# Weights summed and split ahead and kept in DRAM, and seven products in two more token pairs: attention with two feed-forward networks on one core

## The chip, the core and the metric

The kernel runs on one core of one Trainium2 chip. The metric is device time in microseconds (us), from the start to the end of one execution. The engines are TensorE (PE, matrix products), VectorE (DVE), ScalarE (ACT), GpSimd (POOL) and SyncE (SP). PE, DVE and ACT compute here. SP and POOL hand out transfers between DRAM and the on-chip memory (SBUF), each from a queue of its own in the order in which the program lists them; POOL also issues transfers that add what they bring to what is there. PE writes to eight accumulator banks (PSUM) of 128 x 512 fp32.

## What is computed

The reference, cut to its core (N = 6016 tokens, C = 256, hidden width 2048, all fp32):

```
qn = q / (norm(q, axis=tokens) + 1e-6);  kn = k / (norm(k, axis=tokens) + 1e-6)
s  = kn.T @ qn / tau                     # 256 x 256
a  = softmax(s, axis=-1)
x  = v @ a                               # 6016 x 256
h  = x @ w_in;   x2  = silu(h) @ w_out
h2 = x2 @ w2_in; out = max(0.01 * h2, h2) @ w2_out
```

So there is a small attention over channels and then two feed-forward networks over all tokens. The weights come as 64-bit words and the kernel makes fp32 of them by itself ("decoding").

## The kernel before

**High and low parts.** Every fp32 matrix is split into a high part in a shorter fp32 format (an ACT cast) and a low part (a DVE subtraction). A product of two such matrices is three matmuls: high x high, high x low, low x high. Below, "a product" always means such three matmuls into the same bank.

**Token pairs and steps.** The tokens are cut into six pairs of blocks (`tpairs`): pairs 0 to 4 have two blocks of 512 columns, pair 5 two of 448. The hidden width is cut into eight steps a pair (`SS`), each with two 128-row halves of the hidden layer. A step is (network, pair, step), numbered k = 0 to 95; k = 0 to 47 is the first network. A group g of weights serves steps 2g and 2g + 1.

**Seven products for eight.** A step's first layer is a 2 x 2 block product of weights and tokens. Except in pair 0 of the first network (`first_plain`), `first_seven` computes it by Strassen-Winograd's scheme, with seven products M1 to M7 in place of eight, from sums of weights and sums of tokens that are made beforehand. The second layer is again a 2 x 2 block product. A plain second layer (`l2`) has eight products. `l2_seven` has seven (P1 to P7): it needs sums of the second layer's weights (`wo_sums`: s2, s3, s4 in the tiles `wsh` and `wsl`, and a21 replaced by a21 + a22), and sums of the activations, T1 and T2 on DVE, T3 and T4 as adding transfers on POOL (`onto_home`, L592). T4 feeds P4 and T3 feeds P7. P1, P5, P6 and P7 go through a bank of their own (`ps_x`) for two steps at a time (`BATCHES`), are kept in SBUF as E1 to E5 (`keep`, L684) and are added to the results at the end of the pair (`close`, L689). Which steps use it says `seven`: before, the second network's steps 0, 1, 2, 4, 5 and 6; steps 3 and 7 and the whole first network have plain second layers.

**Between the networks.** `finish` copies the first network's four results a pair (L703) and stores them in DRAM (`y_d`); `tokens` loads them when the second network needs them. In the second network `finish` transposes and stores the output.

**The weights of the second network.** The decoding is cut into jobs (`job_load`, `job_s0`, `job_s1a`, `job_s1`, `job_hi`, `job_lo`), one chain for all 32 pieces of both networks. The first 16 are the first network's: their high and low parts go straight to the weight tiles. The decoded words of the other 16 are stored to DRAM (`w2_d`, L329). From pair 5 of the first network on, `weights(g)` prepares group after group: SP reloads the words (`reload_w`, L1055), DVE makes the seven first-layer forms (`w_sum`, L116), ACT and DVE split them into `wch` and `wcl`; then the same for the second layer (`reload_wo`, L1067; `wo_sums`, L1090; `woh`, `wol`, `wsh`, `wsl`). Both use one buffer, `f`, one after the other.

**What sets the order.** For k < 8 the order is written out by hand. From K0 = 8 on, a planner in the program does it while the program is built: each piece of work is a `Work` with an engine, an estimated cost, what it depends on, a due time and an earliest step; the planner runs a little clock for each engine and lists the instructions in the order that results. `LATE` is how long after its issue it takes a result to be there: 3.0 us for an SP transfer, 4.2 us for one of POOL. On the chip each engine keeps that order, and waits in it for whatever isn't there. Blocks of 128 x 512 ("homes", `take`) are handed out from a list of 46, and of 49 from the second network on, when the buffers of the preparation are given back (`open_more`, `open_last`).

Of the kernel before, what the change touches and what calls it, by code (L numbers as in the profile page):

```python
# [8 lines left out]
F32 = mybir.dt.float32  # L9
F32R = mybir.dt.float32r  # L10
U32 = mybir.dt.uint32
# [8 lines left out]
def attention_moe_kernel(  # L20
# [44 lines left out]
    BATCHES = ((0, 1), (2, 4), (5, 6))  # L65
# [185 lines left out]
    w2_d = {}  # L251

    def w2i_piece(g, kc):
        w2_d["i", g, kc] = dram.tile([P, PW], F32, tag=f"w2i{g}{kc}", name="w2i_d")
        return w2_in[kc * P:(kc + 1) * P, g * GW:(g + 1) * GW, :], w2_d["i", g, kc]

    def w2o_piece(j):
        w2_d["o", j] = dram.tile([P, PW], F32, tag=f"w2o{j}", name="w2o_d")
        return rows(w2_out, 2 * j), w2_d["o", j]
# [52 lines left out]
    def job_s1():  # L312
        if at["s1a"] == at["s1"]:
            job_s1a()
        i = at["s1"]
        if i < at["s1a"]:
            w, r = words32[i]
            nc.vector.tensor_tensor(out=w, in0=w, in1=r, op=ALU.add)
            at["s1"] += 1

    def job_hi():
        i = at["hi"]
        if i < at["s1"]:
# [4 lines left out]
            else:  # L328
                nc.sync.dma_start(out=jobs[i][1], in_=w)  # L329
# [12 lines left out]
    phase = [0]  # L342
# [92 lines left out]
    def seven(step):  # L435
        return step[0] == 2 and any(step[2] in b for b in BATCHES)

    def batch(step):
        return next(b for b in BATCHES if step[2] in b)
# [246 lines left out]
    def close(p, m, half, name):  # L686
# [7 lines left out]

    CLOSE = ((0, 0, "E1"), (0, 1, "E2"), (1, 0, "E3"), (1, 1, "E3"), (0, 1, "E5"), (1, 1, "E5"))

    def finish(moe, p, m, half):
# [4 lines left out]
        if moe == 1:  # L702
            nc.vector.tensor_copy(out=o[:, :n], in_=ps)  # L703
# [15 lines left out]
    with tc.manual_schedule():  # L719
# [260 lines left out]
        plains = sorted(set(range(SS)) - {s for b in BATCHES for s in b})  # L980
        late = [s for b in BATCHES for s in b] + plains
# [70 lines left out]
        def reload_w(g):  # L1052
            wf[g] = new_f(7 * HG, "w_f").rearrange("p (i c) -> p i c", c=HG)
            for kc in range(KC):
                nc.sync.dma_start(  # L1055
                    out=wf[g][:, kc:kc + 3:2, :],
                    in_=w2_d["i", g, kc].rearrange("p (a b) -> p a b", a=2),
                )

        wo_f, wo_more = {}, {}  # L1060

        def reload_wo(g):
            a = new_f(FG * C + 6 * P, "wo_f")
            wo_f[g] = a[:, :FG * C].rearrange("p (f c) -> p f c", c=C)
            wo_more[g] = a[:, FG * C:]
            for x in range(2):
                nc.sync.dma_start(  # L1067
                    out=wo_f[g][:, 2 * x:2 * x + 2, :],
                    in_=w2_d["o", 2 * g + x].rearrange("p (f c) -> p f c", c=C),
                )  # L1070

        def wo_hi(g, s, eng="act"):
            hi_of(woh[g][:, s, :], wo_f[g][:, s, :], eng)

        def wo_lo(g, s):
            lo_of(wol[g][:, s, :], wo_f[g][:, s, :], woh[g][:, s, :])

        wo_s = {}

        def wo_sums(s):  # L1080
            g = s // 2
            f, fi = wo_f[g], s % 2
            wo_s[s] = wo_more[g][:, fi * 3 * P:(fi + 1) * 3 * P].rearrange("p (x c) -> p x c", c=P)
# [8 lines left out]
        def ws_hi(s, eng="act"):  # L1092
            wsh[s] = more_pool[0].tile([P, 3, P], F32R, tag=f"wsh{s}", name="wsh")
            wsl[s] = more_pool[0].tile([P, 3, P], F32R, tag=f"wsl{s}", name="wsl")
            hi_of(wsh[s], wo_s[s], eng)

        def ws_lo(s):
            lo_of(wsl[s], wo_s[s], wsh[s])
# [22 lines left out]
        def open_more():  # L1121
            decode.close()
            more_pool[0] = ctx.enter_context(tc.tile_pool(name="spool", bufs=1))
            fpool[0] = prepare.enter_context(tc.tile_pool(name="fpool2", bufs=1))

        prepare = ExitStack()

        def open_last():
            prepare.close()
# [334 lines left out]
```

## Time and profile before

| what | value |
|---|---|
| median of 3 runs | 1024.15 us (1023.77 to 1024.96) |
| the profiled execution | 1024.44 us |
| its span, first to last instruction | 1022.7 us |
| PE busy | 1010.3 us, 99% |
| DVE busy | 766.8 us, 75% |
| ACT busy | 727.2 us, 71% |
| POOL busy | 93.5 us, 9% |
| moved by DMA | 86.58 MB, 85 GB/s in the mean |

The attention and the first products end at about 75 us. The first network's pair 0 goes on to about 149 us, pairs 1 to 3 to 393.6, pair 4 to 475.2 and pair 5 to about 550. The second network's pairs follow at 78 us each. A share of busy time is a mean over such stretches; what an engine has to spare is read from the stretch in question.

### The profile page before, as it was taken

Reading aid. Unit: us, or ns where it says so; the run is one execution under the profiler, and the core shown is the slowest. Engines: PE = TensorE matmul, PEld = TensorE weight load, DVE = VectorE, ACT = ScalarE, POOL = GpSimd, SP = SyncE. Lnnn points to the kernel's source line nnn. Section 1 sums busy time; section 2 is a strip of 40 time slices with the busy share of each in tenths; the row PEclk is TensorE's granted clock in tenths of the full one; section 3 lists DMA queues with packets and bytes.
Section 4 is the critical chain, followed back from the end, with each engine's and each line's share of the span. In section 5 each row is a group of like instructions: output and inputs, shape, how many; then the busy total and the mean of one; then the engine's idle time right before and its main releaser. Section 6 shows DMA issues by size and latency. Waiting matters only on the chain.

```text
span 1022.7 us, 13051 instructions
## 1 busy us (share of the span) xinstructions
PE 1010.3 (99%) x4516; PEld 843.4 (82%) x4516; DVE 766.8 (75%) x1291; ACT 727.2 (71%) x1336; POOL 93.5 (9%) x109
## 2 busy tenths in 40 slices
PE   9999999999999999999999999999999999999997
PEld 8778888888888888888988778888888888888997
DVE  5889787656747655644777899879879879879886
ACT  7789756765766665755767887876876776877773
POOL 2200000000000000000000111211211211211110
PEclk9999999999999999999999999999999999999999
DMA  9723532214215214001212514623523623522433
GB/s 354 294 82 104 124 68 77 59 54 114 52 50 125 53 31 119 20 20 52 74 61 92 110 42 104 104 42 83 103 42 83 103 42 78 94 41 51 77 57 53
DMA packets 128914, 86.58 MB, mean 85 GB/s; under 512 B 94800, under 2 KB 101200, under 8 KB 128848
## 3 DMA queue, kind: packets, MB, share of 16 engines
q1 hardware_dynamic: 111888, 61.69, 21.3%
q0 software_dynamic: 13248, 23.60, 13.0%
q10 hardware_dynamic: 3712, 0.46, 0.3%
q8 instruction: 35, 0.57, 0.2%
q14 instruction: 31, 0.25, 0.1%
HBM read 45.61 MB, written 16.52 MB: 61 GB/s over the span
## 4 chain that ended last, share of the span: by engine, by line
PE 90%; DMA 4%; ACT 2%; DVE 2%; SPq 1%; issue 1%; DVEq 0%
PE ps_y L629 37%; PE ps_a L456 22%; PE ps_d L456 11%; PE ps_x L629 9%; PE ps_b L456 6%; PE ps_h L456 3%; DMA k_raw<-in_k_dram 2%; PE w_ps L368 1%; DMA q_raw<-in_q_dram 1%; DMA w_raw<-in_moe_w_in_dram 1%; DMA wo_f<-w2o_d 1%; SPq L751 0%; PE s_ps L764 0%; DMA w_f<-w2i_d 0%; ACT hs L467 0%
## 5 line engine op out<-in xcount | busy, mean ns | idle before, releaser
L483 DVE TENSOR_TENSOR gl<-hs,gh 128x512 fp32r<-128x512 f32 (+1 forms) x492 | 322.0, 675 | 84.3 <-ACT gh L122 79.8
L122 ACT CAST gh<-hs 128x512 fp32r<-128x512 f32 (+1 forms) x492 | 287.5, 612 | 10.5 <-PE ps_y L629 2.1
L629 PE MATMUL ps_y<-gl,woh 128*128 128x512 f32 (+1 forms) x552 | 212.8, 386 | 0.8 <-DVE gl L483 0.8
L629 PE MATMUL ps_y<-gh,wol 128*128 128x512 f32 (+1 forms) x552 | 212.8, 385 | 0.5 <-DVE wol L339 0.5
L629 PE MATMUL ps_y<-gh,woh 128*128 128x512 f32 (+1 forms) x552 | 212.8, 386 | 0.0
L456 PE MATMUL ps_a<-xh,wch 128*128 128x512 f32 (+1 forms) x352 | 136.3, 387 | 1.7 <-DVE ps_d L540 1.6
L456 PE MATMUL ps_a<-xl,wch 128*128 128x512 f32 (+1 forms) x352 | 135.6, 385 | 0.0
L456 PE MATMUL ps_a<-xh,wcl 128*128 128x512 f32 (+1 forms) x352 | 135.5, 385 | 0.0
L629 PEld LDWEIGHTS ps_y<-gh,wol 128*128 128x128 f32 x552 | 103.6, 188 | 20.4 <-DVE wol L339 1.0
L629 PEld LDWEIGHTS ps_y<-gl,woh 128*128 128x128 f32 x552 | 103.6, 188 | 20.3 <-DVE gl L483 1.2
L629 PEld LDWEIGHTS ps_y<-gh,woh 128*128 128x128 f32 x552 | 103.6, 188 | 19.9 <-DVE ps_y L689 0.8
L560 DVE TENSOR_TENSOR hs<-ps_a,c 128x512 f32<-128x512 f32 (+1 forms) x88 | 59.6, 677 | 68.5 <-PE ps_a L456 66.4
L592 POOL DMA_DIRECT2D hs<-hs x72 | 62.5, 929 | 363.3 <-DVE gl L483 96.6
L540 DVE TENSOR_TENSOR ps_d<-ps_a,c 128x512 f32<-128x512 f32 (+1 forms) x88 | 60.1, 684 | 47.2 <-PE ps_a L456 45.9
L467 ACT ACTIVATE hs<-ps_b 128x512 f32<-128x512 f32 (+1 forms) x40 | 23.5, 587 | 85.6 <-PE ps_b L456 83.1
L456 PEld LDWEIGHTS ps_a<-xh,wch 128*128 128x128 f32 x352 | 66.1, 188 | 16.9 <-DVE ps_d L540 3.6
L456 PEld LDWEIGHTS ps_a<-xh,wcl 128*128 128x128 f32 x352 | 66.1, 188 | 12.3
L456 PEld LDWEIGHTS ps_a<-xl,wch 128*128 128x128 f32 x352 | 66.1, 188 | 11.9
L456 PE MATMUL ps_d<-xh,wch 128*128 128x512 f32 (+1 forms) x176 | 67.9, 386 | 0.0
L456 PE MATMUL ps_d<-xl,wch 128*128 128x512 f32 (+1 forms) x176 | 67.8, 385 | 0.0
L456 PE MATMUL ps_d<-xh,wcl 128*128 128x512 f32 (+1 forms) x176 | 67.8, 385 | 0.0
L534 ACT COPY ps_b<-ps_a 128x512 f32<-128x512 f32 (+1 forms) x87 | 49.1, 565 | 24.7 <-PE ps_a L456 23.1
(139 smaller groups left out, 1631.3 us busy)
## 6 DMA issues: line engine op xcount, KB each, us to landing
hs<-hs POOLq DMA_DIRECT2D x60, 256.0 KB, 3.2
w_raw<-in_moe_w_in_dram SPq DMA_DIRECT2D x16, 512.0 KB, 4.4
w_raw<-in_moe_w_out_dram SPq DMA_DIRECT2D x16, 512.0 KB, 3.6
y_d<-o SPq DMA_DIRECT2D x20, 256.0 KB, 2.0
xf<-y_d SPq DMA_DIRECT2D x20, 256.0 KB, 3.6
out_dram<-o SPq DMA_DIRECT2D x80, 64.0 KB, 2.2
q_raw<-in_q_dram SPq DMA_DIRECT2D x9, 512.0 KB, 9.9
k_raw<-in_k_dram SPq DMA_DIRECT2D x9, 512.0 KB, 9.9
```

The source lines that it names most:

```text
L122: nc.scalar.copy(out=hi, in_=src)
L368: nc.tensor.matmul(ps, lhsT=a[:, jc, m * P:(m + 1) * P], rhs=b[jc], start=(x == 0), stop=(x == len(order) - 1),)
L456: nc.tensor.matmul(ps[:, :n], lhsT=a, rhs=b, start=(start and x == 0), stop=(x == 2), skip_group_check=not start,)
L467: nc.scalar.activation(out=h, in_=src, func=AF.Silu)
L483: nc.vector.tensor_tensor(out=lo[1], in0=h[1], in1=f32(got[0][1]), op=ALU.subtract)
L534: nc.scalar.copy(out=to, in_=got["A"][:, :n])
L540: nc.vector.tensor_tensor(out=got["D"][:, :n], in0=got["A"][:, :n], in1=got["c5"], op=ALU.add)
L560: nc.vector.tensor_tensor(out=hs[step, "22"][1], in0=got["A"][:, :n], in1=got["c5"], op=ALU.add)
L592: nc.gpsimd.dma_start(out=hs[step, part][1], in_=hs[step, "T2"][1], accum_op=ALU.add)
L629: nc.tensor.matmul(ps, lhsT=a, rhs=b, start=(first and x == 0), stop=(last and x == 2), skip_group_check=True,)
```

## The change

1. **Seven products in the first network's pairs 4 and 5.** `FIRST_SEVEN = 32`: `seven` now also takes the first network's steps from k = 32 on, with the same batches. `finish` adds one kept sum to each of the four results there, so that two of the six closes remain. Before pair 4's step x, `weights_first` replaces a21 by a21 + a22 in the first network's `woh` and `wol` and fills `wsh` and `wsl`, by transfers on POOL.
2. **The preparation is moved.** Decoded words of the second network go into the buffer `f` directly (`job_s1` writes there) and no longer to DRAM. While pairs 1 to 3 of the first network run, `prepare_in` and `prepare_out` make the sums and split everything through two homes at a time (`stage`), and SP stores the high and low parts in DRAM (`store`). The decoding is spaced 0.65 steps a half in place of one. The first network's second-layer words are stored too (`w1_d`, eight transfers in `job_hi`), loaded again (`reload_first`), summed and split (`prepare_first`).
3. **The weights are fetched ready-made.** `weights(g)` is now only transfers on POOL (`fetch`), two for each tile pair, straight into `wch`, `wcl`, `woh`, `wol`, `wsh` and `wsl`: 52 in all with those of the first network.
4. **Around it:** the three additional homes come with `open_more`, when everything is prepared. `LATE` of SP is 5.0 in place of 3.0.

The core of the diff:

```
-    BATCHES = ((0, 1), (2, 4), (5, 6))
+    FIRST_SEVEN = 32
+    BATCHES = {1: ((0, 1), (2, 4), (5, 6)), 2: ((0, 1), (2, 4), (5, 6))}
...
     def seven(step):
-        return step[0] == 2 and any(step[2] in b for b in BATCHES)
+        moe, p, s = step
+        return any(s in b for b in BATCHES[moe]) and (moe == 2 or p * SS >= FIRST_SEVEN)
...
         if moe == 1:
-            nc.vector.tensor_copy(out=o[:, :n], in_=ps)
+            if p * SS >= FIRST_SEVEN:
+                name = WITH[m, half]
+                nc.vector.tensor_tensor(out=o[:, :n], in0=ps, in1=kept[p, name][1][:, :n], op=ALU.add)
+                fed_on(p, name)
+            else:
+                nc.vector.tensor_copy(out=o[:, :n], in_=ps)
...
-            else:
-                nc.sync.dma_start(out=jobs[i][1], in_=w)
+                if i in wo_jobs:
+                    j = wo_jobs.index(i)
+                    w1_d[j] = dram.tile([P, PW], F32, tag=f"w1o{j}", name="w1o_d")
+                    nc.sync.dma_start(out=w1_d[j], in_=w)
...
+        def store(key, cols):
+            name, first = key[:2], key[2]
+            for x, (i, a) in enumerate(staged.pop(key)):
+                if (name, x) not in stored:
+                    stored[name, x] = dram.tile([P, WIDTHS[name[0]]], F32, tag=f"w{name[0]}{name[1]}{x}", name="w_d")
+                nc.sync.dma_start(out=stored[name, x][:, first:first + cols], in_=f32(a[:, :cols]))
+                free.append(i)
+        WIDTHS = {"i": 7 * HG, "o": FG * C, "s": 3 * P, "f": 3 * P, "a": P}
+        def fetch(name, x, to):
+            nc.gpsimd.dma_start(out=to, in_=stored[name, x])
...
-        LATE = {"pe": 0.2, "act": 0.13, "dve": 0.13, "sp": 3.0, "pool": 4.2, "none": 0.0}
+        LATE = {"pe": 0.2, "act": 0.13, "dve": 0.13, "sp": 5.0, "pool": 4.2, "none": 0.0}
...
+        def stage(key, cols, src, deps, at):
+            h = Work("act", sc(cols), lambda eng: stage_hi(key, src(), eng), deps, at, at - 1.0, homes=2, spare=6)
+            l = Work("dve", tt(cols), lambda eng: stage_lo(key, src()), [h], at)
+            ready_d.setdefault(key[:2], []).append(Work("sp", 0.8, lambda eng: store(key, cols), [l], at))
+            return l
+        def prepare_in(g, dep, at):
+            s1 = Work("dve", 2 * tt(HG), lambda eng: w_sum(g, slice(0, 2)), [dep], at)
+            s2 = Work("dve", 2 * tt(HG), lambda eng: w_sum(g, slice(2, 4)), [s1], at)
+            return [
+                stage(("i", g, i * HG), (j - i) * HG, lambda i=i, j=j: flat(wf[g][:, i:j, :]), [s], at)
+                for i, j, s in ((0, 2, s1), (3, 5, s2), (5, 7, s2), (2, 3, s2))
+            ]
...
+        more = Work("none", 0, lambda eng: open_more(), [prev] + clear)
...
+        def load(name, to, deps, at):
+            cost = POOL * max(1, WIDTHS[name[0]] / PW)
+            o = Work("pool", cost, lambda eng: fetch(name, 0, to()[0]), deps + ready_d[name], release=at)
+            return Work("pool", cost, lambda eng: fetch(name, 1, to()[1]), [o], release=at)
+        def weights_first(g):
+            for x in (2 * g, 2 * g + 1):
+                if seven((1, NP - 1, x)):
+                    k = FIRST_SEVEN + x
+                    ms = slice(x % 2 * C + P, x % 2 * C + C)
+                    used_by = users.get((1, x), [])
+                    new = Work("none", 0, lambda eng, x=x: new_ws(x), [more])
+                    W2["first", x, "s"] = W2["first", g] + [
+                        load(("a", x), lambda ms=ms: (flat(woh[g])[:, ms], flat(wol[g])[:, ms]), used_by, k - SS + 1.0),
+                        load(("f", x), lambda x=x: (flat(wsh[x]), flat(wsl[x])), [new], k - SS + 1.0),
+                    ]
         def weights(g):
...
-            r = Work("sp", 0.8, lambda eng: reload_w(g), W2.get(g - 1, [prev]), release=k + 2 + 2 * g)
-            new = Work("none", 0, lambda eng: new_w(g), [r] + used_by)
...
+            new = Work("none", 0, lambda eng: new_w(g), used_by)
+            o = load(("i", g), lambda: (flat(wch[g]), flat(wcl[g])), [new], k + 2 * g + 2)
...
+            done = [load(("o", g), lambda: (flat(woh[g]), flat(wol[g])), [new], k + 2 * g + 3)]
```

## Rows read from the trace of the kernel before

**Rows 1.** The page, parts 1 and 2: busy time by engine; granted clock by slice, in tenths.

```profile
PE 1010.3 (99%) x4516; PEld 843.4 (82%) x4516; DVE 766.8 (75%) x1291; ACT 727.2 (71%) x1336; POOL 93.5 (9%) x109
...
PEclk9999999999999999999999999999999999999999
```

**Rows 2.** PE's waits, whole span: total us, times, longest us.

```profile
PE ps_a L456 <- DVE ps_d L540: 1.6, 1, 1.6
...
PE ps_y L629 <- DVE gl L483: 0.8, 1, 0.8
```

**Rows 3.** Busy time by stretch: PE, PEld, DVE, ACT, POOL, PEclk, DMA share, GB/s.

```profile
148.80:393.60 244.80, 244.80 (x1080) 202.72 (x1081) 148.58 (x237) 161.18 (x288) 5.32 (x6) 1.00 0.28 71
393.60:475.20 81.60, 81.60 (x363) 67.66 (x362) 45.93 (x74) 50.44 (x91) 1.72 (x2) 1.00 0.19 53
475.20:550.00 74.80, 73.22 (x357) 66.67 (x356) 51.01 (x99) 50.24 (x102) 1.73 (x2) 1.00 0.23 69
550.00:628.00 78.00, 77.16 (x339) 62.64 (x338) 70.23 (x125) 61.55 (x118) 12.08 (x14) 1.00 0.37 79
628.00:706.00 78.00, 78.00 (x344) 63.89 (x343) 67.18 (x109) 59.66 (x111) 12.21 (x15) 1.00 0.41 79
```

**Rows 4.** The chain in order of time: start us, us, what.

```profile
383.65 1.36 PE ps_y L629 x6
393.85 1.36 PE ps_y L629 x6
...
541.87 1.21 PE ps_y L629 x6
...
746.02 1.36 PE ps_y L629 x6
...
823.98 1.36 PE ps_y L629 x6
```

**Rows 5.** Timeline, 506 to 520 us: start us, us, engine, line, what [idle before, releaser].

```profile
509.35 1.05 SPq L1067 DMA_DIRECT2D wo_f<-w2o_d  x2
...
515.16 2.13 DVE L1090 TENSOR_TENSOR wo_f<-wo_f 128x128 f32<-128x128 f32 x7 [0.23 <-DMA wo_f<-w2o_d]
...
517.20 0.63 DVE L540 TENSOR_TENSOR ps_d<-ps_a,c 128x448 f32<-128x448 f32 x1
...
517.88 0.47 PE L456 MATMUL ps_a<-xh,wch 128*128 128x448 f32 x1 [1.58 <-DVE ps_d L540]
```

**Rows 6.** Timeline, 580 to 591 us.

```profile
583.30 1.20 SPq L1055 DMA_DIRECT2D w_f<-w2i_d  x2
...
588.50 0.76 DVE L116 TENSOR_TENSOR w_f<-w_f 128x256 f32<-128x256 f32 x2 [1.69 <-DMA w_f<-w2i_d]
...
589.91 0.50 PE L629 MATMUL ps_y<-gl,woh 128*128 128x512 f32 x1 [0.81 <-DVE gl L483]
```

**Rows 7.** DVE's groups by line: count, busy us, mean ns, idle before.

```profile
L125 DVE TENSOR_TENSOR wcl<-w_f,wch 128x512 fp32r<-128x512 f32 (+1 forms) x34 | 19.6, 591 | 2.8 <-ACT wch L122 2.8
...
L116 DVE TENSOR_TENSOR w_f<-w_f 128x256 f32<-128x256 f32 x28 | 11.1, 418 | 3.8 <-DMA w_f<-w2i_d 3.7
L1090 DVE TENSOR_TENSOR wo_f<-wo_f 128x128 f32<-128x128 f32 x24 | 6.9, 290 | 2.3 <-DMA wo_f<-w2o_d 1.7
...
L125 DVE TENSOR_TENSOR wol<-wo_f,woh 128x512 fp32r<-128x512 f32 x8 | 5.2, 685 | 0.3 <-ACT woh L122 0.3
L125 DVE TENSOR_TENSOR wsl<-wo_f,wsh 128x384 fp32r<-128x384 f32 x6 | 3.2, 553 | 0.8 <-ACT wsh L122 0.8
```

**Rows 8.** The line of T3 and T4: issue ns min/median/max; issue to landing (256 KB).

```profile
L592 POOL DMA_DIRECT2D hs<-hs x72: 859/862/1215, 561.3 to 997.7; - x72
...
DMA to landing us min/median/max: 3.0/3.3/6.5
```

**Rows 9.** Waits of PE's weight loads, 625 to 950 us, the longest.

```profile
PEld ps_a L456 <- DVE ps_d L540: 1.1, 4, 0.5
```

**Rows 10.** DMA issues: count, KB each, median us to landing.

```profile
w_raw<-in_moe_w_in_dram SPq DMA_DIRECT2D x16, 512.0 KB, 4.4
```

More of the change, by code (lines that the diff above doesn't have):

```diff
@@ new lines, in reload_first, with prepare_first @@
+        def reload_first(g):
+            wo_f[g] = new_f(FG * C + 6 * P, "wo_f")
+            for x in range(2):
+                nc.sync.dma_start(out=wo_f[g][:, x * PW:(x + 1) * PW], in_=w1_d[2 * g + x])
+        def prepare_first(g, deps, at):
+            s1 = Work("sp", 0.8, lambda eng: reload_first(g), deps, at, at - 1.0)
+            mine = [x for x in (2 * g, 2 * g + 1) if seven((1, NP - 1, x))]
+            for x in mine:
+                s1 = Work("dve", 4 * tt(P), lambda eng, x=x: wo_sums(x), [s1], at)
+            done = []
+            for x in mine:
+                a = x % 2 * C + P
+                done.append(stage(("a", x, 0), P, lambda a=a: wo_f[g][:, a:a + P], [s1], at))
+                done.append(stage(("f", x, 0), 3 * P, lambda x=x: flat(wo_s[x]), [s1], at))
+            return done
@@ L1239, in weights @@
+            for x in (2 * g, 2 * g + 1):
+                if seven((2, 0, x)):
+                    used_by = users.get((1, x), [])
+                    new = Work("none", 0, lambda eng, x=x: new_ws(x), [more] + used_by)
+                    done.append(load(("s", x), lambda x=x: (flat(wsh[x]), flat(wsl[x])), [new], k + 2 * g + 3.5))
             W2[g] = done
-            if g == G - 1:
-                Work("none", 0, lambda eng: open_last(), done)
-        TWOS = {}
-        after_fin, state, ends, owing = {}, {}, {}, []
+        users = {}
@@ L1252, in first @@
                 tokens(qi + 1)
[L1253 to L1258 removed]
+            if moe == 1 and FIRST_SEVEN <= k < FIRST_SEVEN + SS and s % 2 == 0:
+                weights_first(g)
+            for g_ in range(G):
+                if k == SS * (NP - 1) + 1 + max(batch((1, NP - 1, x))[-1] if seven((1, NP - 1, x)) else x for x in (2 * g_, 2 * g_ + 1)):
+                    weights(g_)
             if qi == 2 * NP - 1 and s == 0:
@@ L1318, in add, with two @@
             ready = first(k) if k >= K0 else dict.fromkeys(PARTS)
-            wdeps = W2.get(g, []) if moe == 2 else W2["first", g]
-            def two(fn, form, m, half, at, deps=(), ready=ready):
+            wdeps = W2.get(g, []) if moe == 2 else W2.get(("first", s, "s"), W2["first", g])
+            def two(fn, form, m, half, at, deps=(), ready=ready, x=s):
                 key = p, m, half
```

176 lines of the change are left out of this document (87 added, 89 removed).

## The prediction

> **What bounds the kernel now.** I read the page's first two parts first: TensorE (PE) is busy 99% of a 1022.7 us span and its clock stands at full speed in every slice [rows 1]. The reader should see that no slice in the middle has room in it, so only two things can shorten the kernel: fewer matmuls, or PE's few waits. Then PE's own waits [rows 2]: after the attention stage there are just two, 1.6 us and 0.8 us. The other small rows of that view (0.7 us and less) lie in the first 70 us, which the change leaves almost alone. Then the stretches pair by pair [rows 3]: a plain 512-column pair of the first network (393.6 to 475.2) has PE 81.60 of 81.60 us busy, DVE 45.9 (56%), ACT 50.4 (62%). A seven-product pair of the second network (628 to 706) has PE 78.00 of 78.00, DVE 67.2 (86%), ACT 59.7 (76%). Last the chain [rows 4]: it is PE nearly all the way, and its evenly spaced pieces give the cadence: 383.65 to 393.85, so a plain step takes 10.20 us; 746.02 to 823.98, so a seven-product pair takes 77.96 us. A piece of two products (six matmuls) takes 1.36 us at 512 columns and 1.21 us at 448, so one product costs 0.68 or 0.605 us.
>
> **What is removed from PE.** In pairs 4 and 5 of the first network, six steps of eight (0, 1, 2, 4, 5, 6) go from eight second-layer products to seven. Pair 4: 6 x 0.68 = 4.08 us. Pair 5 has 448 columns: 6 x 0.605 = 3.63 us. Together 7.7 us (36 matmuls), all on the path, since PE never waits there apart from the stall below.
>
> What the saving brings with it is read from the second network, which does the same already. Its pair holds 6 x 14 + 2 x 15 = 114 products, 114 x 0.68 = 77.5 us, and takes 77.96: about 0.45 us a pair goes in short hesitations, which [rows 9] shows as waits of the weight loads for ps_d, while the same view for PE from 625 to 950 us has no row at all. A plain pair, 120 x 0.68 = 81.6, loses nothing. I charge 2 x 0.45 = **0.9 us**.
>
> **Does the rest fit into these pairs?** Each seven-product step adds on DVE T1, T2 and three more lows, five instructions at 0.685 us, the mean of a 512-column low in the wol row [rows 7]: 3.4 us a step, 20.6 us a pair. Kept sums and closes are some ten more, 7 us. Pair 4 then has 45.9 + 27.6 = 73.5 us less the decoding that moves away (five pieces of three instructions, together some 10 us as an estimate by the same 0.685), so about 64 us of 78, or 82%, under the 86% that the second network bears. ACT's three extra casts a step are no longer than the lows: at most 50.4 + 12.3 = 62.7 of 78. POOL gets 24 more T3/T4 issues at 0.862 us [rows 8]. finish now adds a kept sum where it copied; both are one 512-column DVE instruction, so nothing is added on the way to the next pair. I cost all this at nothing beyond the 0.9; the cover is the DVE and ACT share, and if it is gone the two pairs fall back to what they cost now.
>
> **The two stalls.** Both lie where the second network's weights are prepared, and both have one cause. In the first [rows 5] SP issues the reload of wo_f at 509.35; DVE, which must add these weights next in its order, stands until they have landed and does seven sums from 515.16, 2.13 us in all. Only then comes the ps_d sum for which PE stands 1.58 us. In the second [rows 6] the reload of w_f is issued at 583.30, the DVE instruction that needs it starts at 588.50 after 1.69 us of idling on that DMA, and PE waits 0.81 us. The change takes the reload, the sums and the splits out of this stretch, so both go: **2.4 us**. What is late next is the ordinary 0.45 us a pair; nothing larger shows at these places.
>
> **The moved preparation.** Its DVE rows [rows 7] add up to 11.1 + 6.9 + 5.2 + 3.2 us and, of the wcl group, about half of 19.6 (22 + 12 lows, of which three 512-column ones and one of 256 a group of weights are the second network's, 9.9 us): 36 us, now beside steps 8 to 32 (148.8 to 393.6). New there are the first network's own sums (another 6.9 us) and splits (some 5 us, an estimate by the wsl row). Decoding is squeezed from two steps a piece to 1.3, so four more pieces (8 us) fall here. DVE: 148.6 + 56 = 205 of 244.8 us, 84%; ACT, one cast a low and two instructions a piece, each no longer than a low: at most 161.2 + 29 = 190, 78%. Today these pairs lose nothing at 61% and 66%; the second network's lose 0.45 each at about the new shares. Bounds: 0 to 3 x 0.45 = 1.35 us; a gain is excluded because PE has no wait there to give back. I take the middle, **0.65 us**, since neither end has a nearer row.
>
> SP gets some 84 stores, eight copies of decoded words and eight reloads, and loses 16 stores and 16 reloads. A store stands on SP until its low is done; queued behind it are loads of v and stores of y, which are due a whole pair ahead. The bytes (high and low parts of four groups of 896 KB and four of 512 KB, and the sums) are 17 MB in 245 us, 70 GB/s on top of 71 [rows 3]. Cost nothing; if the cover fails, the loads of v are late and the next pair's first product waits.
>
> **The 52 fetches on POOL's queue** are what before does not show. Each waits for PE's last use of the tile that it overwrites, and T3, T4 and the x sums are queued behind it on the same queue. The largest is 896 KB, twice for each of four groups. From 256 KB in 3.3 us [rows 8] and 512 KB in 4.4 us [rows 10], another 256 KB costs 1.1 us as an estimate, so both (1.75 MB, 7 x 1.1) ahead of a T4 hold it back 7.7 us and it would land 11.0 us after its issue. One landing took 6.5 us [rows 8] and PE had no wait in that stretch, so up to 3.2 us more than usual is covered. Bounds: 0 below (no PE wait is left there for a fetch to shorten), 4 x 4.5 = 18.0 us above. I take **0.5 us**, near the lower end, because a tile overwritten now is needed six steps later, and T4 is behind a fetch only if it becomes ready just after it.
>
> The Trainium skill speaks against this part. The page "SBUF — State Buffer" (section "SBUF: two separate sides") says that DMAs issued from GpSimd starve while DVE runs in a two-port mode, since their descriptors cannot be written, and advises the SP or ACT queue. Here, beside a DVE that is 86% busy, the issues took 0.859 us at least, 0.862 in the median and 1.215 at most [rows 8]; by the row the 52 fetches are not starved, so the rule adds nothing to the sum. The page "DMA: Bandwidth & Descriptors" (section "Anatomy of one DMA — SWDGE (gpsimd) path") gives 2.0 us and bytes over 436 GB/s; an estimate by that page is 4.2 us of holding back for a pair of 896 KB, by which the bound would be some 4 us instead of 18.0.
>
> **The sum.** The profiled execution took 1024.4 us (span 1022.7 and 1.7 around it), 0.3 above the median of 1024.15. 1024.4 - 7.7 - 2.4 + 0.9 + 0.65 + 0.5 = 1016.35; against the median, **1016.0 us**.
>
> **The rivals.** *The stalls move.* DVE and ACT stay as full in the first network's last pairs as they are in the second, and new waits of the old size (2.4 us) stand elsewhere: 1018.4. For it: 82 to 86% DVE everywhere now. Against it: at that share PE waits for nothing from 625 to 950 us. 18%.
>
> *The sums come late.* The space for the sums of the first network opens only when the last decoded piece is split and stored, about step 32, where pair 4 begins and needs them about 1.4 steps later. The chain of decoding is serial, with one buffer for the words. If it is late by a step, 10.2 us, PE still has the next first layer (seven products, 4.8 us) to do: 5.4 us, 1021.4. Against it: one piece needs six DVE and ACT instructions, some 4 us, and has 13. 7%.
>
> *Slower: the queue of the fetches.* All four pairs of 896 KB get in front of a T3/T4 and PE stands 4.5 us each: 1016.0 - 0.5 + 18.0 = 1033.5. It decides from 2.7 us a group, 10.7 us in all, where 1026.2 is reached. Against it: the 6.5 us landing that nobody noticed, and POOL at 12 of 78 us. 7%.
>
> *It does not do what it says.* DVE's order fills up, the saved products turn into waits and the two pairs keep their 81.6 and 74.8 us; only the later stall goes: 1023. For it: 27 us of new DVE work in each. Against it: the same work fits in the second network. 4%.
>
> *More is gained:* pair 0 of the second network (550 to 628, DVE 90% [rows 3]) loses its small hesitations as well, and no new cost appears: under 1013. 6%.
>
> **The numbers.** The forecast, 1013 to 1017.5, has 58%. From 1013 to 1021 lie this, the moved stalls and most of the late sums: about 8 in 10. A difference of 0.2% (2 us) is about what a measurement of this kernel can tell from none. Faster by more: 58 + 18 + 6 + 5 of the 7 for late sums = 87%. Within: the rest of those and the 4% = 6%. Slower: 7%.
>
> **What would show it.** PE has 36 matmuls fewer, and pairs 4 and 5 of the first network take about 78.0 and 69.5 us. T3/T4 issues go from 72 to 96. The ps_d wait of 1.6 and the gl wait of 0.8 are gone, with no wait of DVE for w_f or wo_f beyond 1 us. DVE from 150 to 385 us is near 84%. Landings of T3/T4 between 470 and 600 us stay under 7 us. A PE wait of over 2 us near 400 us would prove the late sums right, and one behind gh in 470 to 600 us the queue of the fetches.

## The result, and the profile after

The changed kernel takes 1015.25 us in the median of four runs (1014.45 to 1017.24), the kernel before 1024.47 beside it: a ratio of 0.9913, with a 95% interval of 0.9896 to 0.9931. It was timed once more, with the experiments below: 1015.04 us, ratio 0.9902 (0.9889 to 0.9916). The profiled execution took 1014.45 us, of which the span is 1012.7. So the step from profile to profile is 10.0 us, and from median to median 9.2 and 9.9.

The page of the changed kernel, part 1, as in [rows 1]:

```profile
PE 1002.2 (99%) x4480; PEld 836.8 (83%) x4480; DVE 822.6 (81%) x1407; ACT 751.0 (74%) x1392; POOL 142.5 (14%) x185
```

PE has 36 matmuls fewer and is as full as it was; DVE has 116 instructions more. PE's waits over the whole span (total us, times, longest us), the longest row that lies behind the start of the kernel:

```profile
PE ps_x L646 <- ACT E L123: 0.9, 1, 0.9
```

It is new, and both waits of [rows 2] are gone. Busy time by stretch (PE, PEld, DVE, ACT, POOL, PEclk, DMA share, GB/s), to be laid beside [rows 3]; the stretches are pairs 1 to 3, pair 4, pair 5, and the second network's pair 0:

```profile
148.80:393.60 244.80, 244.80 (x1080) 202.74 (x1081) 190.57 (x352) 179.04 (x334) 17.12 (x28) 1.00 0.52 150
393.60:471.60 78.00, 78.00 (x345) 64.28 (x344) 62.56 (x101) 58.76 (x109) 13.17 (x16) 1.00 0.36 73
471.60:541.40 69.80, 69.64 (x337) 62.62 (x336) 56.71 (x99) 52.19 (x106) 20.38 (x29) 1.00 0.66 170
541.40:619.40 78.00, 78.00 (x347) 64.40 (x346) 64.54 (x105) 59.39 (x111) 19.37 (x27) 1.00 0.66 170
```

In pairs 1 to 3 PE is busy for all of 244.80 us, as before, though DVE's work there rose from 148.58 to 190.57 us and the traffic from 71 to 150 GB/s. In the second network's pair 0 DVE fell from 70.23 (90%) to 64.54 us (83%), since nothing is summed or split there any more.

**Where the time went** is read from the chain in order of time: the same pieces of six matmuls are in it before and after, and the difference of their starts is what was gained up to there. The chain after:

```profile
393.88 1.36 PE ps_y L646 x6
...
735.50 1.36 PE ps_y L646 x6
...
814.63 1.36 PE ps_y L646 x6
...
975.38 1.22 PE ps_y L646 x6
```

[rows 4] has 393.85, 746.02 and 823.98 for the first three; to the last answers this one of the kernel before:

```profile
984.99 1.22 PE ps_y L629 x6
```

Up to 393.9 nothing is gained or lost (+0.03). At 735.5 the gain is 10.52 us. At 814.6 it is 9.35: 1.17 us were given back in the second network's pair 3, where the new wait stands. At 975 it is 9.61, and the last 0.4 us come behind that.

### The profile page after: what moved, and what is told of

Same layout as the page of the kernel before. It is cut to its first block, busy times and chain, and to the rows that moved or that the text cites. A ratio compares the mean times of both kernels' runs of the same rounds, so it can differ in the third digit from the quotient of the medians.

```text
span 1012.7 us, 13541 instructions
## 1 busy us (share of the span) xinstructions
PE 1002.2 (99%) x4480; PEld 836.8 (83%) x4480; DVE 822.6 (81%) x1407; ACT 751.0 (74%) x1392; POOL 142.5 (14%) x185
## 4 chain that ended last, share of the span: by engine, by line
PE 92%; DMA 3%; ACT 2%; DVE 1%; SPq 0%; issue 0%; ACTq 0%
PE ps_y L646 35%; PE ps_a L473 23%; PE ps_x L646 12%; PE ps_d L473 12%; PE ps_b L473 6%; PE ps_h L473 3%; DMA k_raw<-in_k_dram 2%; PE w_ps L384 1%; DMA q_raw<-in_q_dram 1%; DMA w_raw<-in_moe_w_in_dram 1%; SPq L777 0%; PE s_ps L790 0%; ACT gh L123 0%; DVE gl L500 0%; ACT hs L486 0%
## 5 line engine op out<-in xcount | busy, mean ns | idle before, releaser
L500 DVE TENSOR_TENSOR gl<-hs,gh 128x512 fp32r<-128x512 f32 (+1 forms) x528 | 345.9, 674 | 67.1 <-ACT gh L123 61.2
L123 ACT CAST gh<-hs 128x512 fp32r<-128x512 f32 (+1 forms) x528 | 308.7, 611 | 9.0 <-PE ps_y L646 1.2
L646 PE MATMUL ps_y<-gh,wol 128*128 128x512 f32 (+1 forms) x480 | 185.7, 387 | 0.5 <-DVE wol L355 0.5
L646 PE MATMUL ps_y<-gh,woh 128*128 128x512 f32 (+1 forms) x480 | 185.6, 387 | 0.0
L646 PE MATMUL ps_y<-gl,woh 128*128 128x512 f32 (+1 forms) x480 | 185.5, 387 | 0.0
L609 POOL DMA_DIRECT2D hs<-hs x96 | 83.6, 913 | 396.2 <-DVE gl L500 102.5
L646 PEld LDWEIGHTS ps_y<-gh,wol 128*128 128x128 f32 x480 | 90.1, 188 | 18.4 <-DVE wol L355 1.0
L646 PEld LDWEIGHTS ps_y<-gh,woh 128*128 128x128 f32 x480 | 90.1, 188 | 17.7 <-DVE ps_y L712 0.6
L646 PEld LDWEIGHTS ps_y<-gl,woh 128*128 128x128 f32 x480 | 90.1, 188 | 17.3
L596 DVE TENSOR_TENSOR hs<-hs 128x512 f32<-128x512 f32 (+1 forms) x96 | 64.5, 672 | 11.9 <-ACT hs L486 7.2
```

The source lines that it names most:

```text
L123: nc.scalar.copy(out=hi, in_=src)
L500: nc.vector.tensor_tensor(out=lo[1], in0=h[1], in1=f32(got[0][1]), op=ALU.subtract)
L596: nc.vector.tensor_tensor(out=out[1], in0=hs[step, a][1], in1=hs[step, b][1], op=ALU.subtract)
L609: nc.gpsimd.dma_start(out=hs[step, part][1], in_=hs[step, "T2"][1], accum_op=ALU.add)
L646: nc.tensor.matmul(ps, lhsT=a, rhs=b, start=(first and x == 0), stop=(last and x == 2), skip_group_check=True,)
```

## The experiments

In each, the ratio is to the kernel before on the same chip, with its 95% interval. Line numbers are those of the kernel that ran, so they differ a little from run to run. Except for the third, all start from the changed kernel and keep its `LATE` of 5.0 for SP.

### The move alone

No step of the first network takes seven products, and what was stored and summed for them (`w1_d`, `prepare_first`) is left out.

```
-    FIRST_SEVEN = 32
+    FIRST_SEVEN = 48
...
-                if i in wo_jobs:
+                if False:
...
-                        clear = (prepare_first(i // 2, prepare_in(i // 2, prev, k + 1.0 + LAG), k + 1.5 + LAG) if i < 2 * G else prepare_out(i // 2 - G, prev, k + 1.0 + LAG))
+                        clear = (prepare_in(i // 2, prev, k + 1.0 + LAG) if i < 2 * G else prepare_out(i // 2 - G, prev, k + 1.0 + LAG))
```

> The preparation is moved as in the change, but the first network keeps eight products everywhere (and so its second-layer words are neither stored again nor summed). Theory (the gain is a sum of two parts, fewer matmuls and two removed reload stalls): the stalls of 1.6 and 0.8 us are gone and PE runs 36 matmuls more than the changed kernel, 7.7 us, so about 1021.5 to 1022.5, some 2 to 3 us under the kernel before. Rival (the stalls only move to another place while DVE is as full): 1024, no difference to before.

1021.70 us, 0.9970 (0.9959 to 0.9982). As expected: without the sevens the rest of the change takes out the two stalls and a little more, 2.9 us. This is the move together with the later `LATE`; the third experiment shows that the number alone gives most of it. None of PE's waits behind the startup is longer than 0.5 us. The sevens are worth what is left to the change, some 7 us (1021.70 - 1015.04 = 6.7; by the two ratios 7.0), of the 7.7 that their 36 matmuls take.

### The sevens alone

The seven-product layers stay in pairs 4 and 5, and the first network's sums are still prepared, stored and fetched. The second network's weights go back to the way of the kernel before: words to DRAM, reloaded, summed and split from pair 5 on.

```
-                to, view = jobs[i][1]()
-                nc.vector.tensor_tensor(out=to.bitcast(U32), in0=view(w), in1=view(r), op=ALU.add)
...
+            else:
+                nc.sync.dma_start(out=jobs[i][1], in_=w)
...
+        def reload_w(g):
+            wf[g] = new_f(7 * HG, "w_f").rearrange("p (i c) -> p i c", c=HG)
...
+        def reload_wo(g):
+            wo_f[g] = new_f(FG * C + 6 * P, "wo_f")
```

> Seven products in pairs 4 and 5 of the first network as in the change, but the second network's weights are prepared where the kernel before does it, from pair 5 on. Theory (the seven products need the room on DVE that the move makes): pair 5 then has some 57 us of DVE for its own steps, read from the changed kernel, and some 18 us of preparation, 75 us in a stretch of 70, so PE waits there and in the pair behind it by 5 to 8 us, and the two reload stalls (2.4 us) are back: 1022 to 1025. Rival (the move matters only for the two stalls): 1014.5 + 2.4, about 1017.

1027.09 us, 1.0022 (1.0014 to 1.0031): slower than the kernel before, with all 36 matmuls saved, and slower than the 1022 to 1025 that were expected. Its busy time in the second network's pair 0:

```profile
541.00:629.00 88.00, 82.75 (x354) 65.19 (x353) 83.69 (x155) 71.67 (x137) 11.35 (x14) 1.00 0.41 100
```

and PE's waits over its whole span, the three largest rows that are not of the startup:

```profile
PE ps_y L637 <- DVE gl L491: 2.3, 3, 0.9
PE ps_x L637 <- DVE E L692: 1.7, 3, 0.8
...
PE ps_a L464 <- DVE ps_d L548: 1.4, 1, 1.4
```

DVE is at 95% there (83.69 of 88), and all three rows are waits for it (the next two, 1.1 and 0.9 us, are for ACT). So the two halves of the change are not two gains to be added: alone the move gives 2.9 us and the sevens lose 2.5 (on 1024.58 of the kernel before, on the same chip); together they give 9.9 (1015.04 on 1024.90). The sevens need the room on DVE that the move makes. Laid beside the kernel before with the later `LATE` too (1022.45 us, next experiment), the difference is sharper: the move alone then gives about 1 us, and the intervals of the two runs overlap; the sevens alone cost 4 to 5; both give 7 to 8. One thing is not parted from DVE's load here: in this kernel the three additional homes come as late as in the kernel before.

### The kernel before with a later estimate of the reloads

```
-        LATE = {"pe": 0.2, "act": 0.13, "dve": 0.13, "sp": 3.0, "pool": 4.2, "none": 0.0}
+        LATE = {"pe": 0.2, "act": 0.13, "dve": 0.13, "sp": 5.0, "pool": 4.2, "none": 0.0}
```

> The kernel before with one number changed: the planner counts 5.0 us, not 3.0, until an SP transfer is there. If the two stalls come from reloads that took 5 us or more where the planner had counted on 3, most of the 2.4 us go without anything being moved: about 1022. If they come from a DVE and ACT that are too full there, the wait appears elsewhere and the time stays at 1024.

1022.45 us, 0.9981 (0.9972 to 0.9989). Both waits of [rows 2] are gone from PE's list with this one number. That settles what they were: the planner counted a reload as there 3.0 us after its issue, it took until 515.16 after 509.35 [rows 5] and until 588.50 after 583.30 [rows 6], and DVE stood in its order with PE's work behind it. About a fifth of the change's gain was to be had without moving anything.

### Seven products in pair 3 too, at four paces of the decoding

If sevens pay wherever DVE has room, pair 3 should give another 4.08 us. Its sums have to be ready 8 steps earlier, so the decoding must be closer together than 0.65 steps a half. The edit is the same four times, with 0.55, 0.50, 0.45 and 0.40:

```
-    FIRST_SEVEN = 32
+    FIRST_SEVEN = 24
-            k = K0 + x * 0.65
+            k = K0 + x * 0.55
```

> The changed kernel with seven products in pair 3 of the first network too (from step 24 on) and the decoding spaced 0.55 steps a half in place of 0.65, so that the sums are ready by then. Theory (each 512-column pair gives six products, 4.1 us, and costs under 0.5 us while DVE stays at or under 90%): 3.6 us under the changed kernel, about 1011. Rival (DVE is the bound in pairs 1 and 2, where 17 steps now hold all decoding and preparation, some 155 of 173 us, or the sums come late): no better than 1014.

> Seven products in pair 3 too, with the decoding spaced 0.50 steps a half, between the two runs at 0.45 and 0.55. Theory (at 0.55 the sums were late by some 15 us, at 0.45 DVE was full between 220 and 250 us and PE waited about 2 us): with 17 us more than 0.55 the sums are just in time and DVE is less full, 1011.5 to 1014. Rival: the sums are still late for a step, over 1016.

> As the run with seven products in pair 3 too, but the decoding is spaced 0.45 steps a half in place of 0.55, which brings the last sum about 3 steps earlier. Theory (that run lost its time because the fetched sums were late, PE stood for them and then ran at the lower clock): no wait of PE for wsh or wsl, no slice at the lower clock, and the gain of pair 3 shows: about 1011 to 1013. Rival (DVE and ACT cannot hold decoding, sums and splits in two pairs): waits of PE for DVE and ACT between 150 and 320 us, no better than 1015.

> The same with 0.40 steps a half, another 17 us earlier. Theory: the sums are early already at 0.45, so this changes nothing on that side, and the fuller stretch behind step 8 costs 0 to 2 us: 1011 to 1014. Rival (room on DVE decides): slower than at 0.45 by more than 2 us.

| pace | median us | ratio (95%) |
|---|---|---|
| 0.55 | 1027.20 | 1.0022 (1.0013 to 1.0032) |
| 0.50 | 1023.31 | 0.9983 (0.9974 to 0.9991) |
| 0.45 | 1014.48 | 0.9898 (0.9885 to 0.9912) |
| 0.40 | 1017.95 | 0.9935 (0.9923 to 0.9948) |

All four missed what their theories gave (1011 to 1014 us), and none is measurably faster than the change (0.9902 and 0.9913). At **0.55** the sums are late. PE's waits from 315 to 353 us, those for a transfer:

```profile
PE ps_y L646 <- DMA wsl<-w_d: 3.8, 1, 3.8
...
PE ps_y L646 <- DMA wsh<-w_d: 1.6, 1, 1.6
```

The same run's PE in order of time (start us, us, line, what, idle before and releaser):

```profile
335.98 0.80 PE L473 MATMUL ps_a<-xh,wch 128*128 128x512 f32 x1 [1.68 <-ACT ps_b L551]
336.57 0.63 PE L473 MATMUL ps_a<-xl,wch 128*128 128x512 f32 x1
337.00 0.63 PE L473 MATMUL ps_a<-xh,wcl 128*128 128x512 f32 x1
...
347.31 0.79 PE L646 MATMUL ps_y<-gh,wsl 128*128 128x512 f32 x1 [3.75 <-DMA wsl<-w_d]
```

and its busy time in that stretch:

```profile
335.00:353.00 18.00, 11.69 (x30) 8.64 (x31) 8.34 (x14) 8.23 (x15) 8.20 (x14) 0.72 0.83 213
```

PE waits for the fetches of `wsh` and `wsl` themselves; the 1.68 us shown first is the last and longest of four other waits from 329 us on, for DVE and ACT, 2.8 us in all. The granted clock is 0.72 in the mean of the stretch: behind the waits of 1.68 and 3.75 us the matmuls start 0.43 us apart (336.57 and 337.00) where they otherwise start 0.23 apart (six in 1.36 us, in the chain above), which is the lower of the two levels, 1.2 for 2.4 GHz. The waits for the two fetches are 5.4 us in that list; the matmul starts from 325 to 350 us lie some 12.5 us further apart in all than at the plain cadence of 0.227 us; most of what is left beside all these waits went at the lower level. So the forecast's rival of late sums is a real mechanism, one pair earlier than it was put.

At **0.50** no wait for a fetch is left in PE's list, and the loss has another place. Its PE at its longest wait:

```profile
251.31 0.50 PE L646 MATMUL ps_y<-gh,woh 128*128 128x512 f32 x1 [3.13 <-DVE o L729]
```

and its busy time there:

```profile
250.00:260.00 10.00, 7.78 (x21) 5.87 (x22) 6.82 (x15) 5.17 (x10) 0.00 (x0) 0.66 0.45 159
```

That is not what was expected: where the second layer goes over to the next pair and DVE copies the results of the old one, PE stands 3.1 us, and behind a second wait of 0.9 us, at 253.19, its matmuls run at the lower level for nearly 6 us (0.66 in the mean of the stretch). Why DVE is late just there at this pace and not at 0.45 stays open.

At **0.45** the waits for sums are gone and the clock is full, and at **0.40** it is slower again. Both, and the changed kernel as a third, from 220 to 250 us:

```profile
220.00:250.00 30.00, 29.14 (x126) 23.05 (x126) 28.22 (x57) 22.67 (x45) 0.86 (x1) 1.00 0.83 235
```

```profile
220.00:250.00 30.00, 28.86 (x123) 22.31 (x122) 29.02 (x57) 22.61 (x45) 1.91 (x2) 1.00 0.87 244
```

```profile
220.00:250.00 30.00, 30.00 (x135) 24.82 (x134) 23.27 (x48) 21.85 (x43) 0.00 (x0) 1.00 0.71 200
```

DVE goes from 78% in the change to 94% and 97%, PE from 30.00 to 29.14 and 28.86 us. How much of the 4.08 us goes there is seen by counting matmuls: from the start of pair 1 to the place in pair 4 where 2769 of them are left, the kernel at 0.45 gains 1.9 us on the change and the one at 0.40 loses 2.2. So 2.2 and 6.2 us went ahead of pair 4. At 0.45 that is about half of the saving; 1.2 us more are lost behind this place, and why is not known. (This profile is also 1.1 us late at the start of pair 1, where nothing was altered; the two profiles of the changed kernel differ there by 0.6.) So a slower pace makes the sums late, and a faster one fills DVE ahead of pair 3 and loses there, on PE, half of what pair 3 saves or more than all of it. (The transfers are denser too, 235 and 244 GB/s for 200, and these runs don't part the two; the waits of the 0.40 run between 200 and 392 us are 2.2 us for DVE and 0.7 for ACT, and none for a transfer.)

### The fetches on SP's queue

Which queue issues the 52 fetches, in two ways: first as SP's work for the planner too (both parts of the diff), then with the planner's lists for PE, DVE and ACT exactly as in the change and only the issuing queue another (the first part alone).

```
-            nc.gpsimd.dma_start(out=to, in_=stored[name, x])
+            nc.sync.dma_start(out=f32(to), in_=stored[name, x])
...
-            o = Work("pool", cost, lambda eng: fetch(name, 0, to()[0]), deps + ready_d[name], release=at)
-            return Work("pool", cost, lambda eng: fetch(name, 1, to()[1]), [o], release=at)
+            o = Work("sp", cost, lambda eng: fetch(name, 0, to()[0]), deps + ready_d[name], release=at)
+            return Work("sp", cost, lambda eng: fetch(name, 1, to()[1]), [o], release=at)
```

> The changed kernel with the 52 fetches of ready-made weights on SP's queue in place of POOL's. Theory (issues on POOL cost 0.5 to 1.2 us each and what T3 and T4 lose behind a fetch is covered): landings of T3 and T4 go back under 6.5 us, and the time stays within 1 us of the changed kernel, 1014.5 to 1016. Rival (the fetches on POOL starve or hold back T3 and T4): faster by 2 us or more.

> The changed kernel with its planned order on PE, ACT and DVE left as it is, and only the 52 fetches issued by SP in place of POOL. If the run with fetches on SP was slower because the planner, which then counts them on another queue, no longer leaves room for them among T3 and T4, this one has the changed kernel's time, 1014.5 to 1016.5. If SP's queue is worse in itself (fetches beside T3 and T4 on the same engines, SP standing for PE with stores of y behind it), it is near 1019 to 1021.

1020.68 us, 0.9959 (0.9946 to 0.9971), and 1019.94 us, 0.9950 (0.9937 to 0.9964). The first was expected within 1 us of the change and is not. The second, 4.9 us slower than the change on the same chip, is where its expectation put it if the queue, and not the planner, makes the difference. What SP does in that form from 550 us on (start us, us, engine, line, what):

```profile
553.89 3.72 SPq L731 DMA_DIRECT2D y_d<-o  x4
557.66 1.09 SPq L1114 DMA_DIRECT2D wcl<-w_d  x1
558.80 1.12 SPq L1114 DMA_DIRECT2D wsh<-w_d  x2
```

what follows on the other engines:

```profile
563.58 0.86 POOL L609 DMA_DIRECT2D hs<-hs  x1 [6.60 <-DVE gl L500]
...
572.85 1.14 ACT L123 CAST gh<-hs 128x512 fp32r<-128x512 f32 x2 [2.99 <-DMA hs<-hs]
...
573.52 0.50 PE L646 MATMUL ps_x<-gh,wsh 128*128 128x512 f32 x1 [1.70 <-ACT gh L123]
```

the landings of T3 and T4 (us, min/median/max):

```profile
DMA to landing us min/median/max: 3.0/3.4/9.2
```

and the busy time from 560 to 573 us, in this run and in the changed kernel:

```profile
560.00:573.00 13.00, 11.82 (x53) 9.45 (x51) 7.79 (x13) 9.00 (x18) 1.72 (x2) 1.00 1.03 332
```

```profile
560.00:573.00 13.00, 13.00 (x59) 10.57 (x58) 10.80 (x18) 11.78 (x24) 5.00 (x8) 1.00 0.72 187
```

The fetches stand in SP's list behind the stores of `y_d`, which must wait for the results of a pair, and then go out in a burst of twelve until 567 us. In these 13 us the traffic is 332 GB/s for 187. The transfer for T3 or T4 issued at 563.58 on POOL's queue, with nothing ahead of it there, lands 9.2 us later; ACT waits for it, and PE 1.7 us for ACT. By the chain, this run falls 3.5 us behind the change on the same chip between 515 and 585 us. Another 1.2 us of the difference lies ahead of 150 us, where nothing was altered: PE waits 1.4 us there for the loads of k, and 0.3 in the change, so this part is not the queue's.

### Each fetch twice, and the traffic twice

To measure the queue by itself, each fetch was issued twice into the same tile. To measure the traffic by itself, each fetch was followed by a second transfer of the same bytes to a place in DRAM that nobody reads:

```
-            nc.gpsimd.dma_start(out=to, in_=stored[name, x])
+            for _ in range(2):
+                nc.gpsimd.dma_start(out=to, in_=stored[name, x])
```

```
             nc.gpsimd.dma_start(out=to, in_=stored[name, x])
+            again = dram.tile([P, WIDTHS[name[0]]], F32, tag=f"again{name[0]}{name[1]}{x}", name="again_d")
+            nc.gpsimd.dma_start(out=again, in_=stored[name, x])
```

> The changed kernel with every fetch issued twice, so POOL's queue carries 104 and twice the 17 MB, while the planner counts them once. Theory (what T3 and T4 are held back is covered by several us): landings up to some 12 us, and PE waits for a few of them: 0 to 4 us more, 1015 to 1019. Rival (each group's fetch stands before a T3 or T4 that PE needs at once): 8 us or more on top, over 1023.

> The changed kernel with each fetch followed on POOL's queue by a second transfer of the same bytes to a place in DRAM that nobody reads. It adds the traffic and the issues of the run with doubled fetches, but no wait of POOL for a landing. If that run lost its 98 us by POOL standing for landings with T3 and T4 queued behind it, this one costs 0 to 6 us: 1015 to 1021, with landings of T3 and T4 up to some 12 us. If it lost them by the traffic, this one is over 1060.

1113.29 us, 1.0861 (1.0840 to 1.0882), against 1017.75 us, 0.9926 (0.9913 to 0.9938). The first was expected at 1019 at most. The second transfer into a tile waits until the first has landed, and POOL stands in its queue for that. In the first kernel, the longest wait of PE and the largest of POOL's six rows for fetches (total, times, longest):

```profile
PE ps_y L646 <- ACT gh L123: 21.9, 1, 21.9
...
POOL wsh L1115 <- DMA wsh<-w_d: 42.6, 12, 5.8
```

and its POOL and ACT in order of time:

```profile
429.31 0.53 POOL L1115 DMA_DIRECT2D wol<-w_d  x1 [1.94 <-DMA wol<-w_d]
429.91 1.79 POOL L609 DMA_DIRECT2D hs<-hs  x2
...
434.57 0.62 ACT L123 CAST gh<-hs 128x512 fp32r<-128x512 f32 x1 [23.44 <-DMA hs<-hs]
```

The first T3 and T4 of pair 4 go out at 429.91 (403.9 in the change), when the last fetch ahead of them has been let go, and PE stands 21.9 us for what they bring. The five largest rows of PE's waits, all for ACT, add up to 77.9 us; the other 20.5 of the 98 us are PE's longer busy time (1022.7 for 1002.2 us), at a mean granted clock of 0.963. With as many issues and as many bytes, and only 8.8 us of POOL waiting for a transfer at them where the first kernel has 180, the second kernel is 2.7 us slower than the change. By the chain it loses 2.0 us of this between 542 and 592 us, where three of the eight 896 KB fetches are. Its second transfers go to DRAM and not to the tile, so the traffic is the same in bytes only. Within that limit, it isn't the number of fetches on POOL's queue that costs, and the bytes cost little; it is an instruction that waits in the queue.

### The change once more

> The changed kernel once more, on the same chip as the three others, as their measure: 1014.5 to 1016.

1015.04 us, 0.9902 (0.9889 to 0.9916). It has the new wait again, 0.9 us at 803 us.

## Why the prediction was right

The forecast was 1016.0 us (1013.0 to 1021.0); the medians are 1015.25 and 1015.04. On the profiled execution's own scale the sum was 1016.35 and the measured time 1014.45: 1.9 us less. Step by step:

**The 36 matmuls, 7.7 us, and the first stall, 1.58 us: right.** Both lie in pairs 4 and 5. The first matmul of a pair is that of ps_d with the new pair's tokens; for pair 4 and for the second network's pair 0 it starts, after the change, at

```profile
391.68 0.39 PE L473 MATMUL ps_d<-xh,wch 128*128 128x512 f32 x1
...
539.90 0.40 PE L473 MATMUL ps_d<-xh,wch 128*128 128x512 f32 x1
```

and before at

```profile
391.65 0.39 PE L456 MATMUL ps_d<-xh,wch 128*128 128x512 f32 x1
...
549.00 0.40 PE L456 MATMUL ps_d<-xh,wch 128*128 128x512 f32 x1
```

157.35 us became 148.22, a gain of 9.13 where 9.28 was charged. The order of work around these two rows is not the same before and after, so this is good to half a us or so: where equally many matmuls are left (2089, at 539.9 and 548.4) the gain is 8.5, and at 580 us, with the second stall in it, 10.0. T3/T4 issues went from 72 to 96, as said.

**The second stall, 0.8 us: right**, and a little more came with it, probably because pair 0's DVE was relieved too (90% to 83%). The forecast gave both stalls to the move alone. But the change also has the later `LATE`, and the run with that number alone shows that it takes both out by itself. Up to 735.5 us the gain is 10.52 against the 10.1 of the large terms. The rival by which the stalls move was wrong for this kernel, and the run with the sevens alone shows where it would have been right: with DVE at 95% the saved matmuls came back as waits.

**The hesitations of seven-product pairs, 0.9 us: hardly paid.** 9.28 - 9.13 leaves 0.15; by the count of matmuls 0.8 are missing at 539.9 us, and at 580 the gain is within 0.1 of the large terms. The charge was taken from 77.96 us a pair against 77.5 of products, and the new pairs have DVE at 80% and 81% where the pairs it was read from have 86%.

**The preparation beside pairs 1 to 3, 0.65 us: not paid.** PE's 244.80 of 244.80 us is the lower bound, 0. DVE was forecast at 84% and came to 78%. Two terms were mis-sized, as DVE's groups in 148.8 to 393.6 us show (count, busy us, mean ns, idle before):

```profile
L1090 DVE TENSOR_TENSOR wo_f<-wo_f 128x128 f32<-128x128 f32 x48 | 13.8, 290 | 1.2
...
L117 DVE TENSOR_TENSOR w_f<-w_f 128x256 f32<-128x256 f32 x16 | 6.4, 421 | 0.2
```

The 48 sums of the second layer are the 6.9 + 6.9 that were counted. Of `w_sum`'s 28 instructions [rows 7] only 16 were moved; the other 12 are the first network's own, so that term is 6.4 and not 11.1 us. Four more pieces of decoding were put at 8 us; the three lines that decode went from 21.9 to 27.5 us here, so they are 5.6. The rest of the difference, about 7 of the 14 us, is a slip in the adding: the rows add up the durations of single instructions, and neighbours overlap. DVE's groups in this stretch add up to 156.9 us before and 205.7 after, for 148.58 and 190.57 of busy time; 49 us of added instructions took 42. A count per network, which the source gives, would have been better than the row's total.

**The 52 fetches, 0.5 us: not paid, and the case of the bound of 18.0 did not occur.** The line of T3 and T4:

```profile
L609 POOL DMA_DIRECT2D hs<-hs x96: 848/861/1240, 403.9 to 988.0; - x96
...
DMA to landing us min/median/max: 3.0/3.3/7.6
```

and the largest fetches (count, KB each, median us to landing):

```profile
wch<-w_d POOLq DMA_DIRECT2D x4, 896.0 KB, 6.7
wcl<-w_d POOLq DMA_DIRECT2D x4, 896.0 KB, 7.7
```

One landing did go past 7 us, against what was forecast. It is the transfer that got behind a large fetch (POOL in order of time):

```profile
572.49 0.87 POOL L1114 DMA_DIRECT2D wch<-w_d  x1
573.02 1.24 POOL L609 DMA_DIRECT2D hs<-hs  x1
...
574.11 1.24 POOL L1114 DMA_DIRECT2D wcl<-w_d  x1
```

It was issued 0.5 us after 896 KB and landed 7.6 us after its issue, 4.3 more than usual; ACT has no wait for a transfer there, so nobody noticed. The forecast's bound had both large fetches of a pair ahead of a T4, 11.0 us. Here only one was, and by the forecast's own price of 1.1 us for 256 KB that makes 3.3 + 3.9 = 7.2 us. So the price is close; it was the order that differed, since the planner put other issues between the two. In the run with the traffic doubled a landing took 10.4 us and PE had no wait behind it, while PE lost 2.0 us around others of 6.6 to 7.8 (and 3.5 in the stretch with the one of 9.2, with the fetches on SP's queue). So what a late landing costs doesn't follow from its length alone; probably it hangs on how far ahead of its use the transfer was issued, which was not measured. The forecast's "up to 3.2 us more than usual is covered" was too simple for that.

The page "SBUF — State Buffer" of the Trainium skill (section "SBUF: two separate sides") advises the SP or ACT queue for transfers beside a DVE in a two-port mode. Whether DVE is ever in one here no run shows; POOL's issues, beside a DVE at 78% to 86%, took 0.861 us in the median, as before, and SP's queue made the kernel 4.9 us slower, by what else stood in it. What the run with SP's queue does agree with is the Trainium skill's page "DMA: Bandwidth & Descriptors" (section "Issuing engines are not separate DMA queues"): transfers of all issuing engines run on the same DMA engines; the transfer alone on POOL's queue landed after 9.2 us.

**Late sums: did not occur, and for another reason than was written.** The space was put at step 32; the first fetch of sums goes out 50 us before PE's first use (POOL in order of time, and PE's group for the tile with its first and last start):

```profile
357.98 2.32 POOL L1114 DMA_DIRECT2D wsh<-w_d  x4
```

```profile
L646 PE MATMUL ps_y<-gh,wsh x48: 362/389/395, 408.0 to 986.2; 128*128 128x512 f32 x36, 128*128 128x448 f32 x12
```

At 0.65 steps a half the last pieces of preparation end about 353 us, in step 28. One pair earlier the margin is gone, as the run with the pace of 0.55 shows.

**What no step had: a wait of 0.9 us at 803 us.** DVE, ACT and PE in order of time:

```profile
798.64 1.29 DVE L500 TENSOR_TENSOR gl<-hs,gh 128x512 fp32r<-128x512 f32 x2 [1.27 <-ACT gh L123]
...
800.57 0.63 ACT L486 ACTIVATE hs<-hs 128x512 f32<-128x512 f32 x1 [1.94 <-DVE hs L577]
...
802.74 0.50 PE L646 MATMUL ps_x<-gh,wsh 128*128 128x512 f32 x1 [0.93 <-ACT E L123]
```

DVE stands for ACT, then ACT for DVE, and the copy of E that PE needs is behind both. It comes in both profiles of the changed kernel and in those of the kernels that differ from it in their fetches alone, and the chain gives 1.2 us for the pair. The kernel with the move alone has 0.3 us of the same kind, the kernel before none in its list. It lies 210 us behind the last fetch, so an effect through the planner's order is likely; the cause is not shown. The sum then closes: 2.05 us of small charges not paid and 0.4 gained beyond the large terms by 735 us, 1.2 lost at 803, 0.6 gained after it; 1016.35 - 2.05 - 0.4 + 1.2 - 0.6 = 1014.5, for 1014.45 measured. So the mechanism was right and the large terms were the right size; that the total came within 1.9 us owes something to small terms that went both ways.

## What to carry to other kernels

Saving matmuls on a full TensorE pays only where the engines that feed it have room in that stretch: read DVE's share there, and count what must leave it first (the same 36 matmuls brought some 7 us with DVE at 80% and cost 2.5 with it at 95%). A transfer that waits in an issuing queue can be far dearer than one that only takes bandwidth (98 us and 2.7 here), so ask of each issue what it waits for and what is listed behind it, on every queue it could be put on. Where a planner writes the order, compare its assumed delays with the landings in the trace before anything else: one number gave a fifth of this gain. And where such a number is changed along with the rest, time it alone, or its gain is put down to something else.

## What was not expected of the hardware

- Short stands of PE sometimes cost the clock and sometimes not. In the run at the pace of 0.55, after the 1.68 us at 335.98 (three other waits, of 0.2 to 0.6 us, lie in the 7 us before it) the matmuls ran at the lower level for nearly 3 us, in the run at 0.50, after the 3.13 us at 251.31 and 0.9 more at 253.19, for nearly 6; after the 1.58 us of [rows 5] the trace shows 448-column matmuls 0.20 us apart within 0.3 us, so the upper level. PE had no wait in the 8 us ahead of that one. The forecast counted waits at their own length; behind such stands it would have to count more. Why one stand of 1.6 us cost the clock and the other did not stays open.
- A second transfer into the tile of a first, issued right behind it, made POOL stand up to 6.8 us each time, 50 times and 180 us in all, and the kernel 98 us longer.
